# A new step order for a fused chunk-attention and feed-forward kernel: whole pairs from the first, and the store of pair 16 ahead of pair 17

## The chip, the cores and the metric

The kernel runs on one core of a Trainium2 chip. Its time is the device time of one execution in microseconds (us); several executions give a median. One execution is also recorded by the hardware profiler, which tells when each instruction ran on the engines: PE (TensorE, matrix products; PEld is its weight load), DVE (VectorE), ACT (ScalarE), POOL (GpSimd, which here only issues loads) and SP (SyncE, which here only issues moves and stores).

## The reference

The inputs are q, k and v of 8 batches, 8 heads, 576 positions and 64 values per head, and four weight matrices. Attention is confined to chunks of 64 positions.

```python
q_c = q.reshape(B, H, nc, chunk, D)          # chunk = 64, nc = 9, D = 64; k_c and v_c alike
scores = scale * np.matmul(q_c, k_c.transpose(0, 1, 2, 4, 3))
scores = scores - np.max(scores, axis=-1, keepdims=True)
attn = np.exp(scores)
attn = attn / (np.sum(attn, axis=-1, keepdims=True) + 1e-09)
out = np.matmul(attn, v_c)                   # then heads are put side by side: x is 4608 x 512
a = x @ w1                                   # 512 x 1024
b = x @ w2
h = a * b @ w3                               # 1024 x 1024
return (h @ w_out).astype(np.float32)        # 1024 x 512
```

## The kernel before

The 4608 tokens are cut into 18 "pairs" of 256 tokens (four chunks of one batch or of two). For each pair q, k and v are loaded by POOL with a cast from float32 to bfloat16, 256 KB each after the cast. Since the two last matrices follow each other without anything between, the kernel multiplies w3 by w_out once, into w3o, and uses this product for all tokens.

All work is cut into steps, and one string, ORDER (line 9), writes out the order of the steps by hand. The loop at its end (lines 400 and 401) calls a function for each word. Every engine keeps its own instructions in that order (`keep_in_program_order`), so a step that waits holds up all later steps of its engine, and engines run past each other only as far as their data and buffers let them. A word is a letter and numbers: `A8.2` is step A of pair 8, part 2. The letters:

- q, k, v (POOL): load of a pair; `q0.0` and `q0.1` are the two halves of the heads. i: a quarter of w1 and of w2, in two loads. h: half of w3, in four loads. o: w_out, in four loads.
- T (DVE, line 177): block transpose of a pair's q (`T4.0`) or k (`T4.1`) into qkT. For pairs from 8 on, G (SP, line 187) then moves two pairs' blocks into qkm with eight SBUF-to-SBUF moves.
- S (PE): scores, 64 small matmuls. E (ACT, line 209): exponential. P (PE): attention times v, 64 small matmuls, with the row sums from a column of ones in vbuf.
- N (DVE, lines 236 and 239): reciprocal and product. X (DVE, lines 251 and 259): transpose into xt, or for pairs from 8 on into xm, which H (SP, line 269) moves into xt with eight moves per two pairs.
- A and B (PE): the products with w1 and w2. For pairs 0 to 3 a step is 8 matmuls of 256 columns of one pair, and part j needs quarter j of w1 or w2; from pair 4 on a step is 4 matmuls of 512 columns and serves two pairs, so A4.x stands for pairs 4 and 5. C (ACT, line 306): copy of A's result to SBUF. M (DVE, line 321): the product of the two, into ab.
- V (DVE, line 362): transposes of w3. W (PE, 16 matmuls) and Z (ACT, line 375): the product w3o.
- O (PE, 16 matmuls of 512 columns): the output of a pair. Y (ACT, line 351): copy to SBUF. Q (SP): the store, 512 KB. For the last pair, 17, step O itself makes three smaller copies and stores (lines 339 to 345).
- D (PE): matmuls of zeros into a PSUM tile that a later step uses.

PSUM is one pool of four tiles of two banks each, which S, P, A/B, W and O share. There are five buffers for q and k, six for v (line 111), and three of ab (line 310). In the order before, the first two pairs are loaded, transposed and computed in halves of four heads, and 32 matmuls of zeros with 64 columns stand in front.

Of the kernel before, what the change touches and what calls it, by code (L numbers as in the profile page):

```python
# [41 lines left out]


# [1 line left out]
def kernel(  # L45
# [35 lines left out]
    consts = ctx.enter_context(tc.tile_pool(name="consts", bufs=1))  # L81
# [3 lines left out]
    msb = ctx.enter_context(tc.tile_pool(name="msb", bufs=2))  # L85
    ps = ctx.enter_context(tc.tile_pool(name="ps", bufs=4, space=bass.MemoryType.PSUM))

    def inorder(ins):
        tc.keep_in_program_order(ins)
        return ins  # L90

    def mm(*a, **kw):
        return inorder(nc.tensor.matmul(*a, **kw))  # L93
# [119 lines left out]
    def do_P(p, hh=None):  # L213


        e = e_t[p]
        for u in range(2):
            if (p, u) not in pv_t:
                pv_t[p, u] = psum("pv")
            pv = pv_t[p, u]  # L220
            for m in range(4):
                if p < 8:
                    for g in range(NB) if hh is None else (2 * hh, 2 * hh + 1):
                        for r in range(2):
                            mm(pv[blk[g], r, m * W:(m + 1) * W],
                               lhsT=e[half[r], u, 2 * g + m % 2, m // 2 * BL:(m // 2 + 1) * BL],
                               rhs=vbuf[p % 6][half[r], u, 2 * g + m % 2, 0:W], start=True, stop=True)
# [54 lines left out]

# [25 lines left out]
    def do_M(p, j):  # L308
        g = p // 2
        if g not in ab_t:  # L310
            ab_t[g] = msb.tile([P, FO, GT], bf, tag="ab", bufs=3, name="ab")
        if p < 4:
            o = ab_t[g][:, 2 * j:2 * j + 2, p % 2 * PT:(p % 2 + 1) * PT]
            view = lambda t: t.rearrange("p (j t) -> p j t", j=2)
        elif p < 8:
            o = ab_t[g][:, j]
            view = lambda t: t
        else:
            o = ab_t[g][:, j].rearrange("p (c s y) -> p s c y", s=2, y=BL)
            view = lambda t: t.rearrange("p (s c y) -> p s c y", s=2, y=BL)  # L320
        inorder(nc.vector.tensor_mul(o, view(a_t.pop((p, j))[:]), view(ps_t.pop((p, j))[:, 1, :])))  # L321
# [66 lines left out]
    def load_half3(i):  # L388
# [43 lines left out]
```

The softmax here doesn't subtract the row's maximum and nothing guards it: scores larger than these inputs give would overflow.

## Time and profile before

| | us |
|---|---|
| median of 5 runs | 252.08 |
| lowest and highest | 250.92, 252.67 |
| the profiled execution, its own time | 252.08 |
| its span, from the first instruction to the last | 250.3 |
| PE busy | 228.8 |
| DVE busy | 154.6 |
| ACT busy | 83.6 |
| POOL busy (issuing loads) | 87.1 |

The span is the sum of what the engines show; the device time is 1.8 us more. The profiled execution stands at the median. Loads move 19.41 MB after the cast, SP's moves and stores 17.31 MB. Most time of a step is known from the table of groups: a matmul of 512 columns follows the last after 0.216 us (64 of them took 13.81 us), a step T takes 1.29 us, M 0.68, C 0.59, Y 1.01.

### The profile page before, as it was taken

Reading aid. Unit: us, or ns where it says so; the run is one execution under the profiler, and the core shown is the slowest. Engines: PE = TensorE matmul, PEld = TensorE weight load, DVE = VectorE, ACT = ScalarE, POOL = GpSimd, SP = SyncE. Lnnn points to the kernel's source line nnn. Section 1 sums busy time; section 2 is a strip of 40 time slices with the busy share of each in tenths; the row PEclk is TensorE's granted clock in tenths of the full one; section 3 lists DMA queues with packets and bytes.
Section 4 is the critical chain, followed back from the end, with each engine's and each line's share of the span. In section 5 each row is a group of like instructions: output and inputs, shape, how many; then the busy total and the mean of one; then the engine's idle time right before and its main releaser. Section 6 shows DMA issues by size and latency. Waiting matters only on the chain.

```text
span 250.3 us, 6392 instructions
## 1 busy us (share of the span) xinstructions
PE 228.8 (91%) x2760; PEld 122.6 (49%) x2760; DVE 154.6 (62%) x236; ACT 83.6 (33%) x116; POOL 87.1 (35%) x116
## 2 busy tenths in 40 slices
PE   3329899999999989999999999999999999999992
PEld 2226688884455444544444444444444444444441
DVE  3465965899979589899998899908530331233000
ACT  2110334231434332534425335153232332331322
POOL 8967836487997253673570000000000000000000
PEclk9999999999999999999999999999999999999999
DMA  7999999999999999999999943754402200400334
GB/s 70 148 167 183 191 184 197 196 161 172 147 169 198 232 227 242 183 214 185 196 217 240 270 106 82 170 148 160 115 3 84 84 0 0 170 0 1 135 119 168
DMA packets 93660, 37.12 MB, mean 148 GB/s; under 512 B 77120, under 2 KB 86592, under 8 KB 93632
## 3 DMA queue, kind: packets, MB, share of 16 engines
q0 software_dynamic: 84736, 19.41, 84.2%
q1 hardware_dynamic: 8896, 17.31, 23.6%
q8 instruction: 22, 0.36, 0.6%
q14 instruction: 6, 0.05, 0.1%
HBM read 38.80 MB, written 9.44 MB: 193 GB/s over the span
## 4 chain that ended last, share of the span: by engine, by line
PE 65%; DMA 23%; POOL 4%; SPq 3%; issue 1%; DVE 1%; ACT 0%; DVEq 0%; POOLq 0%; ACTq 0%
PE ab_ps L93 34%; PE o_ps L93 21%; DMA vbuf<-in_v_dram 13%; DMA qkm<-qkT 7%; PE w_ps L93 6%; SPq L169 3%; DMA qk<-in_q_dram 3%; POOL qk L96 2%; PE s_ps L93 2%; PE pv L93 2%; POOL vbuf L96 1%; DVE qkT L177 1%; POOL w L96 1%; ACT e L209 0%; DVE o_sb L344 0%
## 5 line engine op out<-in xcount | busy, mean ns | idle before, releaser
L93 PE MATMUL ab_ps<-xt,w 128*128 128x512 bf16 (+1 forms) x704 | 130.9, 345 | 0.4 <-issue 0.2
L93 PEld LDWEIGHTS <-w 128*128 128x128 bf16 x704 | 68.2, 99 | 55.2 <-issue 0.5
L321 DVE TENSOR_TENSOR ab<-a_sb,ab_ps 128x512 bf16<-128x512 f32 x72 | 48.9, 680 | 48.6 <-ACT a_sb L306 48.3
L306 ACT COPY a_sb<-ab_ps 128x512 f32<-128x512 f32 x72 | 42.3, 587 | 89.4 <-PE ab_ps L93 87.4
L93 PE MATMUL o_ps<-w3o,ab 128*128 128x512 bf16 (+1 forms) x296 | 63.9, 373 | 0.0
L177 DVE STREAM_TRANSPOSE qkT<-qk 128x1024 bf16<-128x1024 bf16 (+1 forms) x40 | 45.8, 1180 | 11.4 <-DMA qk<-in_q_dram 8.8
L93 PEld LDWEIGHTS <-ab 128*128 128x128 bf16 x296 | 28.5, 98 | 32.3
L96 POOL DMA_DIRECT2D vbuf<-in_v_dram x40 | 33.9, 857 | 17.3 <-DMA qk<-in_k_dram 7.5
L351 ACT COPY o_sb<-o_ps 128x1024 f32<-128x1024 f32 x17 | 17.2, 1014 | 42.2 <-PE o_ps L93 42.2
L239 DVE TENSOR_TENSOR xn<-pv,rc 128x512 bf16<-128x512 f32 x36 | 24.9, 692 | 1.2
L96 POOL DMA_DIRECT2D qk<-in_k_dram x26 | 20.3, 784 | 8.1 <-DMA vbuf<-in_v_dram 4.3
L96 POOL DMA_DIRECT2D qk<-in_q_dram x26 | 20.4, 788 | 7.4 <-DMA qk<-in_k_dram 1.9
L209 ACT ACTIVATE e<-s_ps 128x1024 bf16<-128x1024 f32 (+1 forms) x18 | 17.1, 979 | 8.6 <-PE s_ps L93 8.4
L93 PE MATMUL pv<-vbuf,e 64*32 64x65 bf16 (+1 forms) x832 | 11.2, 202 | 4.3 <-DMA vbuf<-in_v_dram 3.1
L236 DVE RECIPROCAL rc<-pv 128x8 f32<-128x8 f32 x36 | 6.9, 192 | 12.6 <-PE pv L93 12.6
L93 PEld LDWEIGHTS <-e 64*32 64x32 bf16 (+1 forms) x832 | 8.5, 100 | 11.6 <-issue 6.4
L93 PE MATMUL w_ps<-wo,w3T 128*128 128x512 bf16 x64 | 14.2, 379 | 0.0
L96 POOL DMA_DIRECT2D w<-in_moe_w_dram x16 | 11.1, 697 | 8.0 <-DMA vbuf<-in_v_dram 2.2
L259 DVE STREAM_TRANSPOSE xm<-xn 128x512 bf16<-128x512 bf16 x20 | 13.6, 697 | 0.2
L251 DVE STREAM_TRANSPOSE xt<-xn 128x512 bf16<-128x512 bf16 x16 | 11.3, 707 | 0.4
L93 PEld LDWEIGHTS <-qkT 32*64 32x64 bf16 x512 | 5.7, 116 | 11.9 <-DVE qkT L177 9.7
L344 DVE COPY o_sb<-o_ps 128x256 f32<-128x256 f32 x1 | 0.4, 424 | 16.0 <-PE o_ps L93 16.0
(19 smaller groups left out, 45.8 us busy)
## 6 DMA issues: line engine op xcount, KB each, us to landing
out_dram<-o_sb SPq DMA_DIRECT2D x17, 512.0 KB, 2.9
qkm<-qkT SPq DMA_DIRECT2D x40, 128.0 KB, 6.9
vbuf<-in_v_dram POOLq DMA_DIRECT2D x32, 128.0 KB, 10.6
w<-in_moe_w_dram POOLq DMA_DIRECT2D x16, 256.0 KB, 7.7
qk<-in_q_dram POOLq DMA_DIRECT2D x10, 256.0 KB, 7.4
qk<-in_k_dram POOLq DMA_DIRECT2D x10, 256.0 KB, 9.6
xt<-xm SPq DMA_DIRECT2D x40, 64.0 KB, 2.7
qk<-in_q_dram POOLq DMA_DIRECT2D x8, 128.0 KB, 4.9
```

The source lines that it names most:

```text
L93: return inorder(nc.tensor.matmul(*a, **kw))
L96: return inorder(nc.gpsimd.dma_start(dst, src))
L169: inorder(nc.sync.dma_start(dst, src))
L177: inorder(nc.vector.transpose(qkT_t[g][:, :, p % 2, s, heads(h)].rearrange("p e h (y t) -> p h t e y", t=2), qk_t[p][:, s, heads(h)].rearr ...
L209: inorder(nc.scalar.activation(e_t[p][:, :, heads(hh)], s_t[p][:].rearrange("p u (h q) -> p u h q", q=CH)[:, :, heads(hh)], Exp, scale=sca ...
L236: inorder(nc.vector.reciprocal(rc[:], pv[:, :, :, D:W]))
L239: inorder(nc.vector.tensor_mul(xn_t[p][:, u], pv[:, :, :, 0:D], rc.to_broadcast([P, 2, 4, D])))
L251: inorder(nc.vector.transpose(new_xt(g)[:].rearrange("p (o t) -> p o t", o=KO)[:, :, t0:t0 + UT] .rearrange("p o (m y) -> p m o y", y=BL), ...
L259: inorder(nc.vector.transpose(xm_t[g][:, u, :, m].rearrange("p o (c y) -> p c o y", y=BL), xn_t[p][:].rearrange("p u r m d -> p (u r) m d" ...
L306: inorder(nc.scalar.copy(a_t[p, j][:], ps_t[p, j][:, 0, :]))
L321: inorder(nc.vector.tensor_mul(o, view(a_t.pop((p, j))[:]), view(ps_t.pop((p, j))[:, 1, :])))
L351: inorder(nc.scalar.copy(o_sb[:], ps_t.pop(p)[:]))
```

## The change

The string ORDER is written anew, so every engine has another order, and three things around it change:

- Pairs 0 and 1 are no longer cut into halves of heads: `T0.0 T0.1 S0 E0 P0` stand for the halves. Only the first q comes in two loads. POOL's loads come in the order q0 k0 v0 q1 k1 v1 i0 i1 q2 k2 v2 i3 i2 q3 k3 v3 h0 o q4 k4 v4 h1, where before it was q0 k0 v0 q1 k1 i0 v1 q2 k2 i1 v2 i2 i3 q3 k3 v3 o h0 h1 q4 k4 v4.
- There are seven buffers for v and four of ab.
- The 32 matmuls of zeros go; one of 512 columns stays, ahead of P0 (`D2.0.0.1`).
- At the end `Y16 Q16 O17` stands for `O17 Y16 Q16`: the copy and the store of pair 16 come before the three copies and stores of pair 17.

Steps A to M of several groups are now mixed (A14.x with A16.x), their parts come in changed sequence, and steps O are spread among them. The diff, but for the other lines in which `p % 6` becomes `p % 7`:

```diff
--- before.py
+++ after.py
@@ -7,37 +7,36 @@
 ORDER = """
-q0.0 k0.0 q0.1 k0.1 v0 q1.0 q1.1 k1.0 k1.1 i0 v1 q2 k2 i1 v2 i2 i3 q3 k3 v3 o h0 h1 q4 k4 v4
-D0.0.32.64 T0.0.0 T0.1.0 T0.0.1 S0.0 T0.1.1 q5 k5 v5 E0.0 S0.1 E0.1 P0.0 P0.1 T1.0.0 N0.0 T1.1.0
-T1.0.1 S1.0 T1.1.1 q6 k6 v6 E1.0 X0.0 S1.1 N0.1 X0.1 P1.0 E1.1 T2.0 A0.0 T2.1 q7 k7 B0.0 C0.0 P1.1
-v7 M0.0 A0.1 N1.0 B0.1 C0.1 X1.0 S2 N1.1 E2 M0.1 X1.1 P2 A1.0 N2.0 B1.0 X2.0 C1.0 A1.1 N2.1 B1.1
-M1.0 C1.1 X2.1 A2.0 M1.1 B2.0 C2.0 A2.1 M2.0 B2.1 T3.0 C2.1 A0.2 M2.1 B0.2 C0.2 T3.1 q8 k8 v8 A1.2
-M0.2 B1.2 C1.2 S3 M1.2 A2.2 E3 B2.2 C2.2 P3 M2.2 A0.3 N3.0 B0.3 X3.0 C0.3 A1.3 N3.1 B1.3 M0.3 C1.3
-X3.1 A2.3 M1.3 B2.3 C2.3 A3.0 M2.3 B3.0 V0 C3.0 A3.1 M3.0 B3.1 V1 C3.1 A3.2 M3.1 B3.2 C3.2 V2 A3.3
-M3.2 B3.3 C3.3 V3 W0 M3.3 T4.0 W1 Z0 V4 V5 T4.1 q9 k9 v9 W2 Z1 V6 V7 T5.0 S4 Z2 W3 T5.1 q10 k10 E4
-T6.0 T6.1 P4 v10 q11 k11 Z3 S5 N4.0 O0 E5 X4.0 N4.1 X4.1 T7.0 O1 T7.1 Y0 Q0 T8.0 P5 v11 q12 k12 Y1
-S6 T8.1 O2 Q1 E6 N5.0 X5.0 N5.1 X5.1 O3 T9.0 T9.1 Y2 G4.0 P6 v12 q13 k13 A4.0 N6.0 B4.0 G4.1 Y3 X6.0
-N6.1 C4.0 A4.1 X6.1 B4.1 C4.1 M4.0 Q2 S7 Q3 M4.1 A4.2 E7 T10.0 B4.2 C4.2 T10.1 P7 v13 q14 k14 A4.3
-M4.2 B4.3 N7.0 C4.3 A4.4 X7.0 M4.3 B4.4 C4.4 N7.1 A4.5 M4.4 B4.5 C4.5 X7.1 S8 M4.5 S9 E8 A4.6 T11.0
-B4.6 E9 T11.1 P8 v14 q15 k15 C4.6 A4.7 M4.6 G5.0 B4.7 C4.7 N8.0 A6.0 M4.7 B6.0 N8.1 C6.0 G5.1 A6.1
-X8.0 B6.1 M6.0 C6.1 X8.1 P9 v15 q16 k16 A6.2 M6.1 N9.0 B6.2 C6.2 N9.1 A6.3 M6.2 B6.3 C6.3 X9.0 A6.4
-M6.3 B6.4 C6.4 X9.1 A6.5 T12.0 H4.0 B6.5 C6.5 M6.4 A6.6 M6.5 B6.6 T12.1 H4.1 C6.6 S10 S11 M6.6 E10
-A6.7 T13.0 B6.7 E11 P10 v16 q17 k17 T13.1 C6.7 O4 M6.7 G6.0 N10.0 N10.1 X10.0 G6.1 P11 v17 Y4 X10.1
-O5 N11.0 N11.1 Q4 X11.0 X11.1 T14.0 A8.0 H5.0 Y5 B8.0 T14.1 C8.0 A8.1 M8.0 B8.1 H5.1 C8.1 T15.0 A8.2
-B8.2 M8.1 C8.2 T15.1 Q5 A8.3 B8.3 C8.3 M8.2 G7.0 S12 M8.3 S13 E12 A8.4 T16.0 B8.4 E13 G7.1 P12 T16.1
-C8.4 A8.5 B8.5 M8.4 C8.5 N12.0 A8.6 M8.5 B8.6 C8.6 N12.1 A8.7 M8.6 B8.7 C8.7 X12.0 P13 M8.7 A10.0
-X12.1 B10.0 C10.0 N13.0 A10.1 M10.0 B10.1 N13.1 C10.1 A10.2 X13.0 B10.2 M10.1 C10.2 X13.1 S14 S15
-M10.2 E14 A10.3 H6.0 T17.0 B10.3 E15 P14 T17.1 C10.3 A10.4 H6.1 M10.3 B10.4 C10.4 N14.0 A10.5 M10.4
-B10.5 G8.0 C10.5 N14.1 A10.6 M10.5 B10.6 C10.6 X14.0 P15 G8.1 X14.1 A10.7 M10.6 B10.7 N15.0 C10.7 O6
-N15.1 M10.7 X15.0 X15.1 H7.0 S16 Y6 S17 O7 E16 E17 H7.1 P16 Y7 O8 Q6 N16.0 Q7 N16.1 X16.0 X16.1 P17
-Y8 A12.0 N17.0 Q8 B12.0 N17.1 C12.0 A12.1 X17.0 B12.1 M12.0 C12.1 X17.1 A12.2 M12.1 H8.0 B12.2 C12.2
-A12.3 M12.2 B12.3 C12.3 H8.1 A12.4 M12.3 B12.4 C12.4 A12.5 M12.4 B12.5 C12.5 A12.6 M12.5 B12.6 C12.6
-A12.7 M12.6 B12.7 C12.7 O9 M12.7 O10 Y9 Q9 A14.0 Y10 B14.0 C14.0 Q10 A14.1 M14.0 B14.1 C14.1 A14.2
-M14.1 B14.2 C14.2 A14.3 M14.2 B14.3 C14.3 A14.4 M14.3 B14.4 C14.4 A14.5 M14.4 B14.5 C14.5 A14.6
-M14.5 B14.6 C14.6 A14.7 M14.6 B14.7 C14.7 O11 M14.7 O12 Y11 Q11 A16.0 Y12 B16.0 C16.0 Q12 A16.1
-M16.0 B16.1 C16.1 A16.2 M16.1 B16.2 C16.2 A16.3 M16.2 B16.3 C16.3 A16.4 M16.3 B16.4 C16.4 A16.5
-M16.4 B16.5 C16.5 A16.6 M16.5 B16.6 C16.6 A16.7 M16.6 B16.7 C16.7 O13 M16.7 O14 Y13 Q13 O15 Y14 Q14
-O16 Y15 Q15 O17 Y16 Q16 Y17 Q17
+q0.0 q0.1 k0 v0 q1 k1 v1 i0 i1 q2 k2 v2 i3 i2 q3 k3 v3 h0 o q4 k4 v4 h1 T0.0 T0.1 q5 k5 v5 S0 E0
+T1.0 D2.0.0.1 P0 N0.0 T1.1 q6 k6 v6 X0.0 S1 N0.1 E1 X0.1 P1 A0.1 N1.0 N1.1 B0.1 X1.0 T2.0 A0.0 B0.0
+T2.1 q7 k7 v7 C0.0 C0.1 X1.1 S2 M0.0 A1.0 E2 M0.1 B1.0 C1.0 P2 M1.0 A1.3 N2.0 A0.3 N2.1 B1.3 X2.0
+C0.3 C1.3 B0.3 M1.3 A0.2 M0.3 A1.2 T3.0 A1.1 C1.2 T3.1 q8 k8 v8 B1.2 C1.1 C0.2 B0.2 X2.1 S3 M0.2
+B1.1 E3 M1.2 A2.0 M1.1 B2.0 C2.0 P3 M2.0 A2.2 V0 A2.3 C2.2 N3.0 B2.2 X3.0 A2.1 N3.1 B2.1 X3.1 C2.1
+C2.3 B2.3 M2.2 V2 A3.0 A3.1 V3 B3.0 C3.1 M2.3 B3.1 M2.1 W1 T4.0 C3.0 V1 M3.1 M3.0 W0 T4.1 q9 k9 v9
+V6 A3.2 Z0 V7 S4 Z1 B3.2 T5.0 C3.2 W3 V4 V5 T5.1 q10 k10 v10 W2 Z3 M3.2 E4 T6.0 T6.1 q11 k11 S5 Z2
+P4 v11 E5 O0 N4.0 T7.0 N4.1 T7.1 q12 k12 P5 v12 Y0 A3.3 X4.0 Q0 X4.1 O1 C3.3 T8.0 N5.0 N5.1 S6 X5.0
+Y1 B3.3 T8.1 q13 k13 E6 O2 X5.1 M3.3 T9.0 T9.1 A4.0 Y2 B4.0 G4.0 C4.0 A4.1 M4.0 B4.1 C4.1 P6 v13 q14
+k14 G4.1 M4.1 S7 N6.0 A4.2 E7 N6.1 A4.4 Q1 X6.0 A4.3 C4.4 X6.1 C4.2 B4.4 T10.0 C4.3 B4.2 M4.4 A4.7
+M4.2 B4.3 T10.1 C4.7 P7 v14 q15 k15 M4.3 B4.7 N7.0 A4.6 M4.7 B4.6 C4.6 X7.0 A4.5 N7.1 S8 T11.0 B4.5
+E8 O3 T11.1 C4.5 M4.5 G5.0 M4.6 X7.1 P8 v15 q16 k16 Y3 A6.0 G5.1 N8.0 B6.0 N8.1 C6.0 S9 M6.0 A6.2 E9
+Q2 X8.0 B6.2 Q3 X8.1 C6.2 P9 v16 M6.2 A6.5 N9.0 B6.5 C6.5 N9.1 A6.4 X9.0 A6.1 C6.4 X9.1 A6.3 T12.0
+H4.0 B6.1 C6.3 M6.5 B6.4 C6.1 B6.3 H4.1 M6.4 A6.6 M6.1 M6.3 S10 C6.6 S11 T12.1 q17 k17 B6.6 E10 A6.7
+E11 M6.6 B6.7 T13.0 C6.7 P11 O4 N11.0 M6.7 N11.1 T13.1 P10 v17 Y4 O5 G6.0 N10.0 N10.1 X10.0 G6.1
+X10.1 T14.0 A8.6 A8.1 T14.1 C8.6 Q4 Y5 B8.6 T15.0 A8.5 A8.2 X11.0 M8.6 B8.5 C8.2 X11.1 C8.5 B8.1
+C8.1 H5.0 A8.0 M8.1 B8.2 A8.3 M8.2 Q5 B8.0 M8.5 C8.0 H5.1 B8.3 C8.3 M8.0 S12 M8.3 S13 E12 A8.7 T15.1
+A8.4 E13 G7.0 B8.7 C8.7 C8.4 P12 M8.7 B8.4 N12.0 A10.1 G7.1 M8.4 B10.1 C10.1 N12.1 A10.2 M10.1 B10.2
+C10.2 P13 M10.2 A10.6 N13.0 B10.6 C10.6 N13.1 A10.5 M10.6 B10.5 C10.5 S14 M10.5 S15 E14 A10.3 X12.0
+B10.3 X12.1 C10.3 X13.0 E15 O6 X13.1 M10.3 H6.0 T16.0 A10.0 Y6 H6.1 P15 B10.0 C10.0 N15.0 O7 N15.1
+Q6 M10.0 T16.1 P14 Y7 A10.7 N14.0 B10.7 Q7 N14.1 A10.4 T17.0 B10.4 C10.4 T17.1 C10.7 A12.1 B12.1
+M10.7 C12.1 G8.0 A12.0 M12.1 A12.2 M10.4 X14.0 B12.0 G8.1 C12.2 X14.1 C12.0 B12.2 O8 M12.2 M12.0
+X15.0 X15.1 H7.0 A12.5 Y8 A12.4 C12.5 B12.5 C12.4 H7.1 A12.6 M12.5 B12.4 C12.6 B12.6 M12.4 Q8 S16
+M12.6 S17 E16 A12.3 A12.7 E17 B12.3 C12.3 C12.7 P16 M12.3 B12.7 N16.0 O9 M12.7 N16.1 P17 Y9 A14.2
+N17.0 B14.2 Q9 X16.0 C14.2 A14.0 N17.1 B14.0 X16.1 C14.0 M14.2 A14.7 X17.0 O10 X17.1 M14.0 H8.0 O11
+Y10 H8.1 C14.7 Q10 B14.7 Y11 O12 M14.7 Q11 A14.6 B14.6 C14.6 Y12 A14.5 M14.6 B14.5 Q12 C14.5 A16.1
+M14.5 O13 C16.1 A16.0 Y13 B16.1 Q13 B16.0 M16.1 A16.4 B16.4 C16.4 C16.0 A16.3 M16.4 A14.1 M16.0
+C16.3 B14.1 C14.1 A14.3 B16.3 C14.3 B14.3 M16.3 A16.2 M14.1 M14.3 A14.4 A16.5 C14.4 C16.2 B16.2
+B16.5 M16.2 A16.7 B14.4 B16.7 M14.4 A16.6 B16.6 C16.6 C16.5 O14 M16.5 M16.6 O15 Y14 C16.7 Q14 M16.7
+O16 Y15 Q15 Y16 Q16 O17
 """
 
 
@@ -108,7 +107,7 @@
 
     zero = consts.tile([P, 512], bf, name="zero")
     inorder(nc.vector.memset(zero[:], 0.0))
-    vbuf = [consts.tile([P, 2, H, VW], bf, name=f"vbuf{i}") for i in range(6)]
+    vbuf = [consts.tile([P, 2, H, VW], bf, name=f"vbuf{i}") for i in range(7)]
     for t in vbuf:
         inorder(nc.vector.memset(t[:, :, :, D:W], 1.0))
...
-                load(vbuf[p % 6][at * CH:(at + m) * CH, u, :, 0:D],
+                load(vbuf[p % 7][at * CH:(at + m) * CH, u, :, 0:D],
...
@@ -270,13 +269,13 @@
 
     ab_t, ps_t, a_t, o_t = {}, {}, {}, {}
 
-    def do_D(which, p, n, cols):
-
-        d, key = (s_t, p) if which == 0 else (ps_t, (p, 0))
+    def do_D(which, p, j, n):
+
+        d, key = ((s_t, p), (ps_t, (p, j)), (pv_t, (p, 0)))[which]
         if key not in d:
             d[key] = psum("z_ps")
         for _ in range(n):
-            mm(d[key][:, 0, 0:cols], lhsT=zero[:, 0:P], rhs=zero[:, 0:cols], start=True, stop=True)
+            mm(d[key][:, 0, :], lhsT=zero[:, 0:P], rhs=zero[:], start=True, stop=True)
 
     def do_AB(p, j, f, which):
 
@@ -308,7 +307,7 @@
     def do_M(p, j):
         g = p // 2
         if g not in ab_t:
-            ab_t[g] = msb.tile([P, FO, GT], bf, tag="ab", bufs=3, name="ab")
+            ab_t[g] = msb.tile([P, FO, GT], bf, tag="ab", bufs=4, name="ab")
         if p < 4:
             o = ab_t[g][:, 2 * j:2 * j + 2, p % 2 * PT:(p % 2 + 1) * PT]
             view = lambda t: t.rearrange("p (j t) -> p j t", j=2)
```

More of the change, by code (lines that the diff above doesn't have):

```diff
@@ L226, in do_P @@
                                lhsT=e[half[r], u, 2 * g + m % 2, m // 2 * BL:(m // 2 + 1) * BL],
[L227 removed]
+                               rhs=vbuf[p % 7][half[r], u, 2 * g + m % 2, 0:W], start=True, stop=True)
                 else:
@@ L230, in do_P @@
                         mm(pv[half[g], r, m * W:(m + 1) * W], lhsT=e[half[r], u, 4 * g + m, :],
-                           rhs=vbuf[p % 6][half[r], u, 4 * g + m, 0:W], start=True, stop=True)
+                           rhs=vbuf[p % 7][half[r], u, 4 * g + m, 0:W], start=True, stop=True)
     def do_N(p, u):
```

## Prediction

> **What bounds the kernel now.** First the page: busy time, and its forty slices of 6.26 us.
>
> ```profile
> PE 228.8 (91%) x2760; PEld 122.6 (49%) x2760; DVE 154.6 (62%) x236; ACT 83.6 (33%) x116; POOL 87.1 (35%) x116
> ...
> PE   3329899999999989999999999999999999999992
> ...
> DVE  3465965899979589899998899908530331233000
> ...
> GB/s 70 148 167 183 191 184 197 196 161 172 147 169 198 232 227 242 183 214 185 196 217 240 270 106 82 170 148 160 115 3 84 84 0 0 170 0 1 135 119 168
> ```
>
> PE is full from slice 4 on. So only three things can change the time: how much PE does before it is full, the gaps after that, and the tail. Second the timeline of the start, all engines:
>
> ```profile
> 18.48 0.41 PE L93 MATMUL pv<-vbuf,e 64*32 64x65 bf16 x16 [2.04 <-DMA vbuf<-in_v_dram]
> ...
> 19.69 3.59 PE L93 MATMUL ab_ps<-xt,w 128*128 128x256 bf16 x16
> ...
> 23.88 2.56 PE L93 MATMUL ab_ps<-xt,w 128*128 128x256 bf16 x16
> ...
> 28.28 0.70 PE L93 MATMUL pv<-vbuf,e 64*32 64x65 bf16 x64 [1.21 <-ACT e L209]
> ```
>
> P1 waits for v1, which is loaded after i0. Then A0.0 starts at 19.7, and P2 waits 1.2 us for E2, with nothing put between. Third PE's own timeline, for its later gaps:
>
> ```profile
> 135.10 0.93 PE L93 MATMUL s_ps<-qkm 64*64 64x64 bf16 x63 [0.28 <-DMA qkm<-qkT]
> ...
> 163.77 1.07 PE L93 MATMUL s_ps<-qkm 64*64 64x64 bf16 x63 [0.47 <-DMA qkm<-qkT]
> ```
>
> S12 and S16 waited for G's moves. Last the timeline of the end, all engines:
>
> ```profile
> 244.80 1.02 ACT L351 COPY o_sb<-o_ps 128x1024 f32<-128x1024 f32 x1
> 245.46 0.42 DVE L344 COPY o_sb<-o_ps 128x256 f32<-128x256 f32 x1 [16.03 <-PE o_ps L93]
> ```
>
> PE ends at 245.4, and the copy of pair 16 (L351) comes after two of pair 17's copies.
>
> My measure is PE's work in ORDER at full rate: S and P 0.64 each, A or B 0.88 (8 x 0.110 us, 256 columns) or 0.87 (4 x 0.216, 512), O and W 3.45. A step's clock time less the work ahead of it is PE's **lag**. Before: S3 has 17.92 ahead and starts at 39.95, lag 22.0; A/B cost 0.11 to 0.222 per matmul in mixed stretches, so the lag drifts little.
>
> **The Trainium skill.** "TensorE: Matmul & The Clock Gate", Part 1, says that PE starts at half rate and needs about 3.4 us of activity for full rate. The trace agrees in kind: the first 16 matmuls took 224 ns each, the next 16 160, later ones 110 to 115; half rate lasted till about 25.1, 5.4 us after 19.7. I use the trace's 5.4. "DMA: Bandwidth & Descriptors", Issuing engines are not separate DMA queues, says that SP's and POOL's transfers share the same 16 engines. The trace agrees: H's moves landed in a median 6.3 and 6.7 us while loads ran (issued 112 and 129), and in 2.0 after them (162).
>
> **The start.** Removed: three issues by POOL and 31 net matmuls of zeros, 1.9 us of PE while it waits for q0; nothing depends on them, and PE idles afterwards long enough to be slow again, so 0. The seventh memset of vbuf (0.07) and the fourth ab are free. Whole S0 comes some 1 us later than its halves, covered by the wait for weights.
>
> What decides is when loads land. Bytes moved, by the windows view: 114 GB/s for 14 us, then 175 to 20 us, 183 to 25, 192 to 30, giving 1.60, 2.65, 3.56, 4.52 MB; then 179 to 198, giving 8.36 MB at 50. In the old order a load lands when about 0.47 MB more than it and its forerunners has moved (k1 1.31 MB at 15.0, 1.77 moved; w1's i1 2.88 MB at 23.8, 3.34 moved). In the new one v1 is 1.57 MB, 16.5 us; i1's w1 2.36 MB, 21.0; its w2 22.4; k2 3.15 MB, 25.3; v2 27. A0.1 comes first, so PE begins with i1: 21.0 to 22.8 at 224 ns, B0.1 to 24.6, both slow until 21.0 + 5.4 = 26.4, A0.0 and B0.0 to 27.3. T2.1 ends at 25.3 + 1.3, so S2 starts at 27.3 with 6.08 ahead: lag 21.2. A1.0 and B1.0 now stand between S2 and P2 and hide E2 (1.03). Against 22.0 that is 0.8; with the 3.4 us of the skill 1.5. I take **-1.0**; bounds +0.5 (i1 1.5 us later) and -2.5 (whole-head loads move faster than halves).
>
> **The later gaps.** G's two waits, 0.75, should go: **-0.75**. DVE's T, N, X, M and V do not change in number, but DVE ran without a gap from 49.1 to 68.4, so its order matters. New waits, by work and lag 21.2:
> - DVE's V6 waits for h1, now behind q4 k4 v4: 9.18 MB, landing at 56.7 to 57.9 (192 or 164 GB/s from 50 on, the rates before and after). W2 (42.54 ahead, 63.7) needs V6, V7, T5.0, V4, 4.8 us: fits until 58.9. T7.0 wants q7 at 69; q7 was issued at 63.8 and loads take 7: up to 0.6 on DVE and A3.3. Take 0.3.
> - H5 for A10.1: P10 ends at 102.45 + 21.2 = 123.6. DVE then does two N, two X, two T14, T15.0, X11.0, M8.6, X11.1: 9.1 us, 132.8. SP has eight moves at 0.62 and Q5, 138.2; landing 2.7 to 6.7: 141 to 145. A10.1 is due at 121.74 + 21.2 = 142.9. G6 for S12: moves from 123 to 129, 7 to land, 136; due 137.5. G7 for S14: 140 to 145, 2.4 to 6.7 to land; due 150.5. v17's issue falls from 129.0 to 123.6 and q17's and k17's by some 9 us, so loads thin out earlier. Take 0.3.
> - PSUM's four tiles: O0 waits for Z2 and E5, A16.6 and O16 for M, each comes free less than 1 us before it is wanted. Take 0.3.
>
> Together **+0.9**; bounds 0, and +5 if DVE falls behind. The mixing of A14 with A16 adds no work: 0, covered by O steps of 3.45 between them.
>
> **The end.** Before, Q16 starts at 246.3, 512 KB, and lands 2.8 later, 249.1; the span ends 1.2 after. With Y16 and Q16 ahead of O17, Y16 runs at about 242 while O17's matmuls take 3.5, and Q16 is issued at 243. SP is free again (0.4 each) by O17's first store at 244.3. The last store is then pair 17's, 128 KB from 245.9, landing 1.7 later, 247.6: **-1.4**. Bounds -1.5 and -1.0 (it shares the DMA engines and lands in 2.1).
>
> **Sum.** -1.0 - 0.75 + 0.9 - 1.4 = -2.25. The profiled execution's own time is 252.08 (span 250.3 and 1.8 around it), equal to the median, so 249.8.
>
> **Rivals.**
> - Loads decide less than I think: whole heads land sooner, PE starts 1.5 us earlier and no new wait comes: -2.5 - 0.75 - 1.4 = -4.65, 247.4. For it: early slices move 140 GB/s and later ones 190. Against: v and the first q are cut as before. Chance 0.12.
> - No gain but the tail: i1 lands 1 us later, PE's lag is as before, and H5, G6, G7 cost 0.5 each where they took 0.75: -1.4 + 0.75 = -0.65, 251.4. For it: the slacks above are within a microsecond. Chance 0.18.
> - **Slower**: DVE blocked by h1. V6 stands ahead of T5, V4, V5, M3.2; if h1 lands after 58.9, each further microsecond is PE's. With the other terms at -2.25 it is slower by over 0.5% from 62.4 on; at 64 it costs 5.1 and gives 254.9. For it: loads of 44 to 50 us were issued 1.3 us apart because POOL waited for earlier ones. Against: the same bytes landed by 53.7 plus 0.8 MB in the old order. Chance 0.12.
> - That the change doesn't do what it says: every engine keeps the written order, so nothing undoes it; where loads gate, the order still gains nothing, which is the second rival.
>
> **The numbers.** Forecast 249.8, with 0.58 for 248.2 to 250.8. Half a per cent, 1.26 us, is what a measurement of this kernel tells from no change. Faster is the forecast and the first rival, 0.70; same the second, 0.18; slower the third, 0.12. The range leaves a tenth on each side: 247.4 to 253.6.
>
> **What would show it.** Right: first 256-column matmul at 21.0 (20 to 22), S2 at 27.3 with no gap before P2, PE's end near 244.5 of its span, last store a 128 KB one, 3.5 us from PE's end to the span's. Wrong: the first A after 22.5; a gap before W3, W2 or S5 with DVE waiting for w's load; a gap before A10.1 or S14 put down to xt's or qkm's moves; PE's end no earlier than 245.4.

## The result, and the profile after

**Not faster: 0.2% slower, if anything.** The changed kernel takes 251.66 us in the median of 43 runs, the kernel before 251.22 in 80; the ratio is 1.0023, 95% interval 1.0010 to 1.0036. (The kernel before, run against itself, gave 0.9986, so a step of this size is hardly more than noise.) The prediction was 249.8, and faster by more than 0.5%. The forecast of the change itself missed by more than these two times show: -2.25 us forecast, +0.44 found, 2.7 apart. The first five runs of the kernel before (252.08) lay 0.9 us above its later median, which hides a third of that.

Most of these 0.44 us do not lie in what the profile shows. The device time of the changed kernel exceeds its span by 2.13 us on average, with all of 44 executions between 2.07 and 2.19; for the kernel before, run along with the experiments, it is 1.80, between 1.72 and 1.95. The medians of the spans are 249.5 us for the changed kernel and 249.1 to 249.5 for the kernel before. Where the 0.33 us come from stays open: of the runs below, those that keep the five steps C of the changed kernel for which PE waits have 2.12 and 2.13, all others 1.77 to 1.85.

The profiled execution after has a span of 249.2 us and a time of its own of 251.36. The page, its first line, busy time and the slices of 6.23 us, PE, DVE and the bytes:

```profile
span 249.2 us, 6337 instructions
...
PE 225.7 (91%) x2729; PEld 119.3 (48%) x2729; DVE 152.5 (61%) x233; ACT 81.3 (33%) x114; POOL 85.3 (34%) x113
...
PE   0339999899999989999999799999989999999994
...
DVE  2577686979699499698994748778246312152210
...
GB/s 63 166 190 176 191 184 204 176 192 172 160 174 215 199 200 202 200 216 264 171 186 249 259 97 12 158 89 168 129 42 84 76 179 84 84 3 0 0 168 170
```

The 8 that before had in its fifth slice is a 9 now, and the last slice is busier (4 for 2), which is the shorter tail. But an 8 has come in the 8th slice (44 to 50 us), a 7 in the 23rd (137 to 143) and an 8 in the 30th (181 to 187), where PE was full.

PE's own timeline after shows where. Columns: start, duration, engine and line, work, and in brackets the idle time before it with what ended it.

```profile
18.82 5.25 PE L92 MATMUL ab_ps<-xt,w 128*128 128x256 bf16 x32 [0.42 <-DMA w<-in_moe_w_dram]
...
24.44 0.71 PE L92 MATMUL s_ps<-qkT 32*64 32x64 bf16 x64 [0.37 <-DVE qkT L176]
...
35.01 1.03 PE L92 MATMUL ab_ps<-xt,w 128*128 128x256 bf16 x8 [0.29 <-ACT a_sb L305]
...
45.86 4.53 PE L92 MATMUL ab_ps<-xt,w 128*128 128x256 bf16 x40 [1.16 <-ACT a_sb L305]
...
141.41 1.02 PE L92 MATMUL ab_ps<-xt,w 128*128 128x512 bf16 x4 [0.79 <-ACT a_sb L305]
...
143.58 3.61 PE L92 MATMUL ab_ps<-xt,w 128*128 128x512 bf16 x16 [1.15 <-DMA qkm<-qkT]
...
184.99 1.02 PE L92 MATMUL ab_ps<-xt,w 128*128 128x512 bf16 x4 [0.79 <-ACT a_sb L305]
...
225.79 6.20 PE L92 MATMUL ab_ps<-xt,w 128*128 128x512 bf16 x28 [0.30 <-ACT a_sb L305]
```

The start is as forecast or better: the first A comes at 18.8, S2 at 24.4, and no gap stands before P2 (before: 1.21). The two gaps at S12 and S16 are gone. Yet six gaps are new. Five end with ACT's a_sb at line 305, which is step C, and the instruction that waits is B0.2, B2.3, B8.4, B12.7 and B16.2. The sixth, 1.15 us, stands before A10.1. The profile names G's moves (qkm) there, but A10.1 reads xt, which H5 fills: the last of H5's moves is issued at 137.8 and lands 5.4 us later, at 143.2, and A10.1 starts at 143.6. (With the five swaps below it is 144.3 and 144.6.) So the wait is read as one for H5. The view of waits sums them up (total, times, longest):

```profile
PE ab_ps L92 <- ACT a_sb L305: 3.3, 5, 1.2
PE ab_ps L92 <- DMA qkm<-qkT: 1.1, 1, 1.1
```

Neither row is among PE's waits in the three profiles of the kernel before, its repetition and its new end alone. The end, on all engines:

```profile
242.43 1.01 ACT L350 COPY o_sb<-o_ps 128x1024 f32<-128x1024 f32 x1 [2.48 <-PE o_ps L92]
...
245.92 0.42 DVE L343 COPY o_sb<-o_ps 128x256 f32<-128x256 f32 x1 [8.21 <-PE o_ps L92]
```

Pair 16's copy (L350) now starts 3.5 us ahead of the last one. PE ends at 245.8, so the tail is 3.4 us, where before it was 250.3 - 245.4 = 4.9.

**The theory** was then: start and tail bring what they should, and two things in the middle eat it. (1) In the old ORDER every C stands behind its own B. In the new one 29 stand ahead of it (`C8.7 C8.4 P12 M8.7 B8.4`), and the program then makes B wait for C, though C reads bank 0 of their PSUM tile and B writes bank 1. (2) A10.1 is held by H5's eight moves, between which SP has the store Q5. **The rivals**: the gaps only show slack that PE would have lost anyway; or the loss lies in the new start.

### The profile page after: what moved, and what is told of

It is laid out like the page before. It is cut to its first block, busy times and chain, and to the rows that moved or that the text cites. A ratio compares the mean times of both kernels' runs of the same rounds, so it can differ in the third digit from the quotient of the medians.

```text
span 249.2 us, 6337 instructions
## 1 busy us (share of the span) xinstructions
PE 225.7 (91%) x2729; PEld 119.3 (48%) x2729; DVE 152.5 (61%) x233; ACT 81.3 (33%) x114; POOL 85.3 (34%) x113
## 4 chain that ended last, share of the span: by engine, by line
PE 84%; POOL 5%; DMA 5%; issue 2%; ACT 2%; DVE 1%; SPq 0%; DVEq 0%; POOLq 0%
PE ab_ps L92 48%; PE o_ps L92 25%; PE w_ps L92 6%; DMA qk<-in_k_dram 3%; PE pv L92 3%; PE s_ps L92 3%; POOL qk L95 2%; ACT a_sb L305 2%; POOL vbuf L95 1%; DMA qkm<-qkT 1%; POOL w L95 1%; DVE qkT L176 1%; SPq L168 0%; DVE o_sb L343 0%; DVEq L343 0%
## 5 line engine op out<-in xcount | busy, mean ns | idle before, releaser
L92 PE MATMUL ab_ps<-xt,w 128*128 128x512 bf16 (+1 forms) x704 | 132.6, 344 | 5.7 <-ACT a_sb L305 3.3
L320 DVE TENSOR_TENSOR ab<-a_sb,ab_ps 128x512 bf16<-128x512 f32 x72 | 47.8, 681 | 63.1 <-ACT a_sb L305 35.5
L305 ACT COPY a_sb<-ab_ps 128x512 f32<-128x512 f32 x72 | 41.1, 589 | 89.7 <-PE ab_ps L92 87.7
L176 DVE STREAM_TRANSPOSE qkT<-qk 128x1024 bf16<-128x1024 bf16 x36 | 45.9, 1298 | 8.0 <-DMA qk<-in_q_dram 7.1
L350 ACT COPY o_sb<-o_ps 128x1024 f32<-128x1024 f32 x17 | 17.2, 1014 | 43.7 <-PE o_ps L92 41.7
L238 DVE TENSOR_TENSOR xn<-pv,rc 128x512 bf16<-128x512 f32 x35 | 24.2, 692 | 1.2
L208 ACT ACTIVATE e<-s_ps 128x1024 bf16<-128x1024 f32 x18 | 18.2, 1029 | 17.4 <-PE s_ps L92 17.3
L95 POOL DMA_DIRECT2D qk<-in_q_dram x25 | 19.7, 788 | 9.8 <-DMA qk<-in_k_dram 2.6
L95 POOL DMA_DIRECT2D qk<-in_k_dram x24 | 18.9, 789 | 7.2 <-DMA vbuf<-in_v_dram 4.0
L92 PE MATMUL s_ps<-qkT 32*64 32x64 bf16 x512 | 6.5, 204 | 11.8 <-DVE qkT L176 11.8
L92 PE MATMUL pv<-vbuf,e 64*32 64x65 bf16 (+1 forms) x800 | 10.1, 199 | 2.1 <-ACT e L208 1.1
```

What stands on the lines that cost most here:

```text
L176: inorder(nc.vector.transpose(qkT_t[g][:, :, p % 2, s, heads(h)].rearrange("p e h (y t) -> p h t e y", t=2), qk_t[p][:, s, heads(h)].rearr ...
L208: inorder(nc.scalar.activation(e_t[p][:, :, heads(hh)], s_t[p][:].rearrange("p u (h q) -> p u h q", q=CH)[:, :, heads(hh)], Exp, scale=sca ...
L238: inorder(nc.vector.tensor_mul(xn_t[p][:, u], pv[:, :, :, 0:D], rc.to_broadcast([P, 2, 4, D])))
L305: inorder(nc.scalar.copy(a_t[p, j][:], ps_t[p, j][:, 0, :]))
L350: inorder(nc.scalar.copy(o_sb[:], ps_t.pop(p)[:]))
```

## The experiments

How far apart do two executions of one kernel lie? The kernel before, run again, is the measure.

> The kernel before once more, for a second profile and for the noise of a comparison. The first profile of before showed a device time near the top of its runs, so both theories expect a ratio of 1.000 within 0.003. If the first profile was typical, the span is again 250 and PE's lag at S3 22.0; if it was a late execution, the span is near 249 and the lag at S3 about 21, with loads landing earlier.

Measured: 250.92, ratio 0.9986 (0.9968 to 1.0004), span 248.1 where the first profile had 250.3. The span of one profile says little to within 2 us, and the first was a late one: k1's second half landed at 15.0 us in it, at 13.8 in the repetition. So medians of many runs decide below, and profiles only say where. PE's lag (as the prediction defines it) at S3 was 22.0, 20.8, 21.8 and 21.2 in the four profiles with the old start, mean 21.5.

### The end alone

```diff
-O16 Y15 Q15 O17 Y16 Q16 Y17 Q17
+O16 Y15 Q15 Y16 Q16 O17
```

> The kernel before with only its last words changed: Y16 Q16 O17 for O17 Y16 Q16. Theory: the prediction's 1.4 us (the profiles of the two kernels show 4.9 and 3.4 us from PE's end to the span's), ratio 0.994. Rival: O17's own copies or stores are held up by Y16 and Q16 and less than 0.5 us is left, ratio over 0.998.

Measured: 249.34, ratio 0.9927 (0.9908 to 0.9946): 0.73% or 1.8 us faster. The tail of its profile is 3.4 us, as in the changed kernel. The end is worth what it was said to be, or somewhat more, and all of the gain is lost elsewhere in the changed kernel.

### The start alone, and its loads alone

On the kernel before: first the new loads and steps up to P1, without any matmuls of zeros, then the old order.

```diff
-q0.0 k0.0 q0.1 k0.1 v0 q1.0 ... P1.0 E1.1 T2.0 A0.0 T2.1 q7 k7 B0.0 C0.0 P1.1
+q0.0 q0.1 k0 v0 q1 k1 v1 i0 i1 q2 k2 v2 i3 i2 ... P1 T2.0 A0.0 T2.1 q7 k7 B0.0 C0.0
```

> The kernel before with the start of the changed one: its order of loads, pairs 0 and 1 whole, no matmuls of zeros, and the rest of the order as before. Theory: the start is worth what the two profiles show, PE's lag at S2 falls from 20.4 to about 18.4 and the time by 2 to 3 us, ratio 0.990. Rival: DVE, not PE, sets the stretch from 49 to 84 us in before, so an earlier start only lets PE wait there, and under 0.8 us is won, ratio over 0.997.

Then only v1 ahead of i0, and i1 ahead of q2:

```diff
-q1.0 q1.1 k1.0 k1.1 i0 v1 q2 k2 i1 v2 i2 i3
+q1.0 q1.1 k1.0 k1.1 v1 i0 i1 q2 k2 v2 i2 i3
```

> The kernel before with one load moved: v1 ahead of i0 (and i1 ahead of q2), the halves of pairs 0 and 1 kept. Theory (the early start of the changed kernel comes from v1 no longer waiting behind weights): P1 is through by 18, the first A at about 18.8 and the lag at S2 falls by 0.5 to 1.5 us against the second profile of before (19.0); ratio 0.995 to 0.998. Rival (it comes from whole heads in one load): lag at S2 as before or later, since A0.0 now waits for i0, ratio 1.000 to 1.004.

Measured: 255.3, ratio 1.0180 (1.0137 to 1.0223), and 253.12, ratio 1.0104 (1.0074 to 1.0135). Both are slower, which neither the theories nor the rivals had foreseen. PE's timeline of the second, and DVE's:

```profile
16.46 3.57 PE L93 MATMUL ab_ps<-xt,w 128*128 128x256 bf16 x16 [0.98 <-DMA w<-in_moe_w_dram]
...
20.52 2.67 PE L93 MATMUL ab_ps<-xt,w 128*128 128x256 bf16 x16
25.82 1.07 PE L93 MATMUL s_ps<-qkT 32*64 32x64 bf16 x64 [2.62 <-DVE ab L321]
28.08 0.75 PE L93 MATMUL pv<-vbuf,e 64*32 64x65 bf16 x64 [1.19 <-ACT e L209]
```

```profile
22.38 1.32 DVE L177 STREAM_TRANSPOSE qkT<-qk 128x1024 bf16<-128x1024 bf16 x1 [6.07 <-DMA qk<-in_q_dram]
23.91 1.31 DVE L177 STREAM_TRANSPOSE qkT<-qk 128x1024 bf16<-128x1024 bf16 x1 [0.21 <-DMA qk<-in_k_dram]
25.12 0.65 DVE L321 TENSOR_TENSOR ab<-a_sb,ab_ps 128x512 bf16<-128x512 f32 x1
```

A0.0 starts 3.2 us earlier than in the first profile of before (19.69), but in the old order the next work (S2) needs pair 2's q and k, which the weights now precede: DVE waits 6.1 us for q2, makes T2.0, T2.1 and then M0.0 (L321), and S2 starts as M0.0 ends. P2 needs E2. With 2.6 and 1.2 us of waiting between so little work PE's clock falls back, here to half from about 25.5 to 32.3 us. In the start alone the waits before S2, P2 and A1.0 are 1.3, 1.2 and 0.9 us. Its windows view, 28 to 34 us (columns: the window, its length, PE, PEld, DVE, ACT and POOL busy, granted clock, DMA share, GB/s):

```profile
28.00:30.00 2.00, 1.29 (x7) 0.93 (x8) 1.93 (x5) 0.00 (x0) 1.04 (x2) 0.64 1.64 191
30.00:32.00 2.00, 2.00 (x11) 1.44 (x10) 1.00 (x3) 0.00 (x0) 0.75 (x2) 0.51 1.91 174
32.00:34.00 2.00, 1.94 (x18) 1.49 (x16) 1.15 (x2) 0.61 (x2) 1.04 (x2) 1.00 2.15 167
```

So the new loads are no gain by themselves. They need the steps that the new order puts up to S3: A1.0 and B1.0 between S2 and P2, and on DVE the steps N1 and X1.0 ahead of T2. Which of these counts for how much was not separated. With them, in the nine profiles with the new order up to S2, that of the changed kernel and eight of those below, the lag at S3 was 18.7 to 20.0, mean 19.5: 2.0 us less than with the old start and the old order.

### C and B

One suspected cost, put on the kernel before eight times over: C14.j ahead of B14.j.

```diff
-A14.1 M14.0 B14.1 C14.1 A14.2
+A14.1 M14.0 C14.1 B14.1 A14.2
```

> The kernel before with C put ahead of its own B in the eight parts of A14, where PE has nothing else to do between A and B. Theory (B waits for C, though C reads one bank of the tile and B writes the other): each costs C's 0.59 us and the two hand-overs, 0.75 to 0.8, less nothing: 6.0 to 6.4 us in all, ratio 1.024. Rival (the banks are told apart, and the waits in the changed kernel have another cause): 0, ratio 1.000.

Measured: 257.73, ratio 1.0265 (1.0225 to 1.0305), +6.7 us. Its waits and two of the eight places on PE:

```profile
PE ab_ps L93 <- ACT a_sb L306: 5.4, 8, 0.7
```

```profile
196.14 1.89 PE L93 MATMUL ab_ps<-xt,w 128*128 128x512 bf16 x8 [0.67 <-ACT a_sb L306]
198.70 1.89 PE L93 MATMUL ab_ps<-xt,w 128*128 128x512 bf16 x8 [0.67 <-ACT a_sb L306]
```

A group of B and the next A, then 0.67 us of idleness, 2.56 us from group to group. PE's lag rises over the eight from 19.2 to 25.8, which is 0.82 each; the displayed gap is smaller than the loss, since the eight matmuls are shown as 1.89 us, though 8 x 0.216 = 1.73 is what they take when the next follows at once. The Trainium skill, "PSUM — Partial Sum Buffer", PSUM bank collisions raise a hardware error, says that accesses of two engines to different banks run clean, and to guard by bank and quadrant. This program guards more coarsely, by the whole tile of two banks, in the order in which it is written: the waits end with ACT's copy in all eight places and in none where C stands behind B. That costs the 0.8. A copy out of one bank beside matmuls into the other was not tried.

Now the cure, in the changed kernel: the five C at which PE waited, put behind their own B (one of the five is shown).

```diff
-C8.7 C8.4 P12 M8.7 B8.4 N12.0
+C8.7 P12 M8.7 B8.4 C8.4 N12.0
```

> The changed kernel with the copy C put after its own B in five places (0.2, 2.3, 8.4, 12.7, 16.2), as it always stands in before. Theory 1: B waits for C whenever C stands ahead of it, since the built program orders them by the whole PSUM tile; PE's five waits for a_sb (0.29 + 1.16 + 0.79 + 0.79 + 0.30 = 3.3 us) go, and the time falls by 2.5 to 3.3 us, ratio to before about 0.99. Rival: PE would meet the next late thing at the same places (evictions, loads), so the waits change their name and less than 1 us is won, ratio 1.000.

Measured: 252.33, ratio 1.0045 (1.0009 to 1.0081). It is no faster than the changed kernel, against the theory in its simple form. The five waits are gone from its trace and the lag at B8.4 is 18.8 instead of 20.5, but then comes this:

```profile
139.72 1.04 PE L92 MATMUL ab_ps<-xt,w 128*128 128x512 bf16 x4
144.61 5.98 PE L92 MATMUL ab_ps<-xt,w 128*128 128x512 bf16 x16 [3.85 <-DMA qkm<-qkT]
```

PE came 1.7 us earlier to A10.1, and waited 3.85 us in place of 1.15. And the 16 matmuls after it took 5.98 us, where they took 3.61 in the changed kernel. The windows view says why (columns as above; the clock stands behind the last bracket):

```profile
142.00:144.00 2.00, 0.00 (x0) 0.00 (x0) 1.00 (x3) 0.00 (x0) 0.00 (x0) 0.65 0.96 188
144.00:146.00 2.00, 1.39 (x4) 0.58 (x5) 0.00 (x0) 0.00 (x0) 0.00 (x0) 0.50 0.99 217
146.00:148.00 2.00, 2.00 (x7) 0.61 (x5) 0.00 (x0) 0.00 (x0) 0.00 (x0) 0.50 0.29 70
148.00:150.00 2.00, 2.00 (x8) 0.77 (x7) 0.69 (x1) 0.58 (x1) 0.00 (x0) 0.64 0.00 0
```

A clock of 0.65 in the first window and of 0.64 in the last means half rate from about 142.6 to 149.4. The Trainium skill, "TensorE: Matmul & The Clock Gate", Part 1, says that the clock is halved after an idle window of about 3.4 us and restored after as much work. The trace agrees that a wait halves the clock and that work restores it, but not in the lengths: here it was half 1.8 us after the last matmul, and full 4.8 us after the first; in the experiment on loads it fell without any wait above 2.6 us.

### What holds A10.1

First with other work put there, O6 and its copy, which in ORDER come later; in the changed kernel alone, with the five swaps, and with all 29 C behind their B.

```diff
-M8.7 B8.4 N12.0 A10.1 G7.1 ... C10.3 X13.0 E15 O6 X13.1 M10.3 H6.0 T16.0 A10.0 Y6 H6.1
+M8.7 B8.4 N12.0 O6 Y6 A10.1 G7.1 ... C10.3 X13.0 E15 X13.1 M10.3 H6.0 T16.0 A10.0 H6.1
```

> The changed kernel with O6 and Y6 moved from before X13.1 to before A10.1: 3.45 us of matmuls whose data are there. Theory (A10.1 stands at a wall that H's moves of pairs 10 and 11 set, about 143 to 144 us after the start, whenever PE comes): the 1.15 us wait goes, and with it the executions in which PE's clock falls to half after the wait; median 1.1 to 1.5 us less than the changed kernel, ratio to before 0.997 to 1.000. Rival (the wait only moves to the place where O6 stood, or to the psum tiles): nothing is won, ratio 1.002.

> Both: C after its own B in the five places, and O6 and Y6 ahead of A10.1. Theory: without the five waits PE comes to A10.1 at about 140.6 us, O6 fills it to 144.0, and at most 0.6 us of wait is left, too short for the clock to fall; lag at the end about 3 us less than the changed kernel's 21.0; time near 248.3, ratio 0.988. Rival: the wall of the moves goes with PE (the moves start when PE has done P10), so PE waits again over 2 us and the ratio stays over 0.996.

> As the kernel with both, but with C after its own B in all 29 places where it stands ahead. Theory: the other 24 cost nothing (PE has other matmuls between), so the ratio is that of the five within 0.003. Rival: a later C delays M and with it the psum tiles, so it is 1 us or more slower than the five.

Measured: 252.27, ratio 1.0052 (1.0032 to 1.0072); 248.29, ratio 0.9901 (0.9869 to 0.9932); 249.09, ratio 0.9917 (0.9891 to 0.9942). So with work to do at A10.1 the five swaps are worth 1.5%. The other 24 C cost nothing measurable: 29 swaps are no better than five. O6 alone gains nothing and may lose 0.3%, against its expectation: the wait before A10.1 is gone, but the five waits stay (3.3 us in its trace), and P15, no longer covered by O6, waits 0.74 us for E15, which it also does in both others.

Then SP's order itself, with the five swaps and without: Q4 and Q5 go from ahead of and between H5's moves to behind G7.1.

```diff
-T14.1 C8.6 Q4 Y5 ... H5.0 A8.0 M8.1 B8.2 A8.3 M8.2 Q5 B8.0 M8.5 C8.0 H5.1 ... A10.1 G7.1 M8.4
+T14.1 C8.6 Y5 ... H5.0 A8.0 M8.1 B8.2 A8.3 M8.2 B8.0 M8.5 C8.0 H5.1 ... A10.1 G7.1 Q4 Q5 M8.4
```

> The changed kernel with C after its own B in the five places, and the stores Q4 and Q5 put behind G7.1 on SP instead of ahead of H5.1. Theory: the wall at A10.1 is SP's order: Q5 stands between H5.0 and H5.1 and waits until Q4 has landed, which holds H5.1's four moves up by about 2 us. Without it they are issued by 136 and land by 142, PE's wait at A10.1 falls from 3.85 us to 1.5 or less, the clock stays full, and the time falls to 248 to 249, ratio 0.988 to 0.992. Rival: the loads still in flight (v17) set the landing; the moves land at 143 to 144 as before, the wait stays over 2.5 us and the ratio over 1.000.

> The changed kernel with one edit: Q4 and Q5 (stores of pairs 4 and 5 on SP) go from between H5's moves to behind G7.1; the five C steps still stand ahead of their own B. This is the fourth corner of a square (neither edit, swap5, this, swap5_stores). Theory: two separate costs that hide each other. A10.1's 1.15 us of waiting for H5's moves goes (0 to 0.3 left), the five waits for ACT's a_sb stay (3.3 us), so about 1.1 us below the changed kernel, 250.5; swap5_stores then gains about 2.4 to 3.3 more from the five swaps. Rival: the order of the stores is the whole matter and the five waits cost nothing once SP is free: about 248.1, as swap5_stores. Second rival: PE comes late enough to A10.1 because of the five waits that SP's order does not matter: 251.5, as the changed kernel, with A10.1's wait put down to something else.

Measured with the swaps: 248.09, ratio 0.9872 (0.9833 to 0.9911); without: 251.09, ratio 1.0005 (0.9989 to 1.0021). SP's timeline in the changed kernel, and that with the stores alone moved:

```profile
131.05 2.54 SPq L168 DMA_DIRECT2D xt<-xm  x4
133.75 0.47 SPq L168 DMA_DIRECT2D out_dram<-o_sb  x1
134.38 4.03 SPq L168 DMA_DIRECT2D xt<-xm  x4
```

```profile
130.30 6.48 SPq L168 DMA_DIRECT2D xt<-xm  x8
```

The last of H5's moves is issued by 136.8 instead of 138.4, and lands at 141.0 instead of 143.2. It is not the half microsecond of issuing a store that makes the difference, nor does Q5 wait until Q4 has landed, as the expectation had it. In the sixteen profiles no transfer of SP is issued before the one eight places ahead of it has landed: that holds in all 1247 cases where both times are on record, in 157 of them the issue follows the landing within 0.1 us, and the one seven places ahead is often still under way. Q4 stands eight places ahead of H5's seventh move. In the run with O6 alone Q5 was issued at 136.05, Q4 landed at 138.45 and H5's seventh move was issued at 138.47; in the fastest kernel below it was 134.00, 137.03 and 137.05. So a store of 512 KB that takes 8 to 10 us to land among the loads holds up the move eight places behind it. With Q4 and Q5 away, G6's moves stand there, which land earlier. Q4 and Q5 were moved together, so their shares are not known.

A10.1's wait is gone with the stores moved, and with the stores alone the five waits stand in the trace unchanged:

```profile
46.51 4.53 PE L92 MATMUL ab_ps<-xt,w 128*128 128x256 bf16 x40 [1.16 <-ACT a_sb L305]
...
141.54 4.48 PE L92 MATMUL ab_ps<-xt,w 128*128 128x512 bf16 x20 [0.79 <-ACT a_sb L305]
```

The square is complete. Medians in us, each cell from its own set of runs; since a clock that falls belongs to the cause here, the runs whose mean clock was below 0.9945 are counted:

| | SP as changed | Q4, Q5 behind G7.1 |
|---|---|---|
| C as changed | 251.66, low clock in 7 of 44 | 251.09, in 0 of 22 |
| five C behind B | 252.33, in 9 of 9 | 248.09, in 0 of 4 |

With SP's order mended the five swaps are worth 3.0 us in the medians, against 3.3 us in the view of waits; between the two ratios, 1.0005 and 0.9872, it is 1.33%, and their intervals together allow 0.9 to 1.8%. About 0.33 us of it lie outside the span. So the gaps were no slack that PE would have lost anyway. With SP's order as it was the swaps are worth nothing: in the profile PE then stands longer before A10.1 and loses its clock, and all nine runs show the low clock. The stores alone are worth 0.6 us in the medians, where 1.1 was expected, and this is not clear of noise: the ratios to the kernel before, 1.0023 and 1.0005, have intervals that overlap. The seven runs of the changed kernel at low clock took 253.2 to 256.1 us; the others had a median of 251.45. Where these seven lost their clock was not seen, since no profile of one was kept; that none of the 44 runs with either O6 or the stores moved shows it points to A10.1.

### What else is to be had

The fastest parts together: five swaps, O6 ahead of A10.1, and E15 right behind E14, against P15's 0.74 us.

```diff
-S14 M10.5 S15 E14 A10.3 X12.0 B10.3 X12.1 C10.3 X13.0 E15
+S14 M10.5 S15 E14 E15 A10.3 X12.0 B10.3 X12.1 C10.3 X13.0
```

> The kernel with the five C after B and O6 ahead of A10.1, and E15 moved ahead of C10.3 on ACT. Theory: the wait of P15 for E15 (0.74 us), which appeared when O6 no longer stood between them, goes; 0.5 to 0.8 us less than without, ratio to before 0.987. Rival: P15 then waits for its psum tiles and nothing is won, ratio 0.990.

In the next, X1.1 ahead of T2.0 and A1.0 ahead of S2 are added to it.

```diff
-B0.1 X1.0 T2.0 A0.0 B0.0 T2.1 q7 k7 v7 C0.0 C0.1 X1.1 S2 M0.0 A1.0 E2
+B0.1 X1.0 X1.1 T2.0 A0.0 B0.0 T2.1 q7 k7 v7 C0.0 C0.1 A1.0 S2 M0.0 E2
```

> As the kernel before this one, with X1.1 ahead of T2.0 on DVE and A1.0 ahead of S2 on PE. Theory: A1.0 (0.88 us) fills the 1.4 us that PE waited for T2.1, so another 0.5 to 0.9 us goes, ratio 0.984. Rival: E2 is then covered by B1.0 alone and P2 waits for it, so under 0.3 us is left of it.

In the last, E15's place is tried with Q4 and Q5 moved instead of O6.

> swap5_stores with E15 right behind E14 on ACT. Theory: in swap5_stores P15 shows no wait for e, since O6 stands ahead of it, so E15's place is worth nothing there (248.1, within 0.3 of swap5_stores). Rival: what made best1 1.4 us faster than swap5_o6 was not P15's 0.74 us wait but ACT's order after it (the C steps behind E15 come otherwise): then it gains here too, 247.0.

Measured, in this order: 246.94, ratio 0.9826 (0.9795 to 0.9857), the lowest median of all and 1.7% below the kernel before. The second: 248.26, ratio 0.9872 (0.9843 to 0.9901): S2's gap shrinks from 0.74 to 0.16 us, P2 gets one of 0.23, A10.1's wait grows from 0.36 to 0.81, and the spans are alike (245.7 and 245.8), so it gains nothing. The third: 247.70, ratio 0.9867 (0.9835 to 0.9900), the same as without E15's move (0.9872): where O6 covers P15, E15's place is worth nothing, as expected. In the first P15's gap is gone, but its profile also stood 1.3 us better at S3 than that of the swaps with O6, and the 1.35 us between their medians is more than the 0.74; the rest was not settled.

## Why the prediction was wrong

It forecast the right start and the right end, and missed the middle.

- **The start, -1.0**: right in sign, too small. Lag at S3 fell by 2.0 us in the means. A0.1 came at 18.8 instead of 21.0 and S2 at 24.4 instead of 27.3: the load times drawn from the old order's bytes were 2 us late for the new one, as the first rival had it. The 5.4 us of half rate were those of one profile too: in the changed kernel the matmuls of 256 columns follow at 0.21 us for 3.3 us from the first A on and then at 0.11, in the repeated kernel before it is about 3.5 us. By the prediction's own sum that is 0.7 of the difference. That E2 would be hidden by A1.0 and B1.0 was right (no gap before P2), and in the experiment with the start alone, which lacks these two steps there, P2 waits 1.2 us for E2 again.
- **G's waits, -0.75**: both are gone. The sizes were those of one execution; in the repeated profile only one stood there, 0.42.
- **The later gaps, +0.9: the step that failed.** From S3 to the end the lag of the changed kernel rises by 2.1 (18.9 to 21.0), where in the repeated kernel before it falls by 2.4 (20.8 to 18.4): 4.5 us, against 0.9 - 0.75 = 0.15 forecast for the same stretch. (Against the first profile of before, where it falls by 1.4, it is 3.5.)
  - *"PSUM's four tiles 0.3"* and *"The mixing of A14 with A16 adds no work: 0"*: mis-sized. The prediction asked when each tile comes free for the next use, and not whether two users of the same tile had changed places. Five B behind their own C cost 3.3 us in the view of waits and, with SP's order mended, 3.0 in the medians.
  - *"H5 for A10.1 ... take 0.3"*: 1.15 us in the profile. The chain was worked out with Q5 in it and A10.1 due at 142.9 between landings of 141 and 145, so the place and the time of H5's last issue (138.2 forecast, 138.4 seen) were right, the latter by luck: the prediction knew only DVE and 0.6 us for each issue, not the landing of Q4, for which the seventh move waited. What was missing is that PE arriving earlier only waits longer, and may lose clock as well: after the 1.15 us of the changed kernel's profile the clock stayed full, after 3.85 us it was half. An earlier start was counted in full, although its gain had to pass this place.
  - *V6 and h1, G6, G7*: no wait of PE at any of them; 0 instead of 0.3 and of their share. With that the slower rival falls.
- **The end, -1.4**: right, 1.5 in the profile (4.9 to 3.4) and 1.8 by itself.

In profiles, against the repeated kernel before: start -1.9, middle +4.5, end -1.5, together +1.1, which is 249.2 - 248.1. The outcome is that of the second rival, "no gain but the tail" (251.4), but not its mechanism: the start did gain, and of its three waits only H5's came. Two of the signs named for a wrong forecast appeared, the gap before A10.1 and a PE end after 245.4.

What stays open: PE stands still once between 90 and 95 us in fifteen of the sixteen profiles, old order or new, for 0.1 to 1.5 us, with nothing that the profile shows as the releaser. It is one reason why single spans do not add up as the medians do.

## What to carry to other kernels

When an order is rewritten, list for every buffer the pairs of users that have changed places, not only the distance between uses: a copy set ahead of the matmuls that share its tile makes them wait for it if nothing else stands between: 0.3 to 1.2 us in five places here, nothing measurable in 24 others. Before you count a gain early in a kernel, look for the next place at which the bound engine waits for something that does not depend on it; the gain ends there. Mend such places together, since one alone may show nothing. In a queue of transfers look eight places ahead of the one you wait for, not only at its neighbours.

## What the hardware showed that was not expected

- A wait of PE can cost more than its length. After 3.85 us of it, the next 16 matmuls of 512 columns took 5.98 us instead of 3.61, so 2.4 us were added. Shorter waits close together do the same: gaps of 2.6 and 1.2 us in the experiment on loads came with a mean clock of 0.985. The clock was half for about 3.4 us in the start alone and for twice that in the two others; 6.8 us at half rate is a loss of 1.4% of the span, which is the mean clock of 0.986 in the profile of the five swaps.
- SP had at most eight transfers under way: none of 1247 was issued before the one eight places ahead had landed, so one slow store delays a small move far behind it.
- The same program moved by 2 us in the span of its profile (250.3 and 248.1), while its median moved by hardly more than 1 us; a mechanism is read from a profile, its worth from medians.
